# Seven block products in place of eight for the attention output of three tile groups, in a two-layer linear-attention and squared-ReLU kernel on one core

## The chip, the cores and the metric

The kernel runs on one core of a Trainium2 chip. The metric is device time in microseconds (us); lower is better. The time of a version is the median of several runs. Work is spread over TensorE (PE; its weight loads are shown apart as PEld), VectorE (DVE), ScalarE (ACT), GpSimd (POOL), and SyncE (SP), which issues nearly all DMAs.

## What is computed

```python
for layer in range(2):                                  # x: 2048 x 640, float32
    q, k, v = heads(layernorm(x) @ wqkv)                # 32 heads of 20
    pq, pk = phi(q), phi(k)                             # phi(t) = where(t > 0, t + 1, exp(t)) + 1e-6
    kv, z = sum_s(pk * v), sum_s(pk)                    # per head
    x = x + ((pq @ kv) / (pq @ z + 1e-6)) @ wo
    h = relu(layernorm(x) @ w1 + b1) ** 2               # 640 -> 1728
    x = x + h @ w2 + b2                                 # 1728 -> 640
```

## The kernel before, in words

The 2048 rows are 16 tiles of 128 rows; four tiles are a **group** g (four groups). Every float32 matrix is kept as a high and a low part, so each block of a matrix product is three matmuls of 128x128 on the weight side: high by low, low by high, high by high.

**First part of a layer.** A loop over the tiles t (lines 823 to 959) computes k and q features and collects, in PSUM, the sum G of x-transposed times k over all tiles. The strips of G for tile t-1 are worked off inside iteration t by `gs(n)` (line 883): line 894 does two of them right after the first block of features of tile t, and they need `kh` of tile t-1, the low half of which is written by DVE at line 793. In layer 0, lines 829 to 834 also store the split weights of k and q to DRAM (`keep_kq`, ten stores of 640 KB) in iterations 11 to 15; layer 1 loads them again. After the loop, G, the block-diagonal per-head kv and wo are multiplied into one 640x640 matrix **M**, kept as five row chunks `M[0..4]` of 128 rows. The attention output of a tile is then P_t @ M, where P_t is pq of the tile divided by its denominator.

**Second part: groups.** For each group, `fc1(g, c)` (line 1189) runs for c = 0..13, each 15 matmuls with 512 moving columns (10 for c = 13), and `act` (line 1210) makes relu squared on ACT. Then 28 `fc2_step`s follow (line 1273): seven block products of a Strassen-Winograd scheme, `ORDER`, of four steps each. Step n reads the n-th unit of the arena, a ring of five slots: ACT writes its high half (`u_hi`, line 1254), DVE the low half (`u_lo`, line 1261), one step after ACT, three steps ahead of PE. DVE also makes the sums of quadrants (`s_op`) and adds the products to the rows (`fc2_add`, line 1295).

**What sets the order.** Work beside the matmuls is put into `events` by hand: `at(g, n, f)` runs f after place n of group g, where n < 14 is an fc1 and n = NF + s an fc2 step s; `("pe", c)` runs PE work right after fc1(c). Each engine works its own queue off in that order. While group g runs, `single(g, i)` (line 1352) prepares tile t = 4(g+1)+i, one of the next group. With b = `OUTS[i]` (4, 7, 10, 13): load pq (`b_load_pq`, place b-8), denominators (`b_den`, b-6: a product and a reduction on DVE), division and transpose (`b_blocks`, b-5), sixteen small block moves on ACT (`blocks_move`, line 449: eight at b-5 and eight at b-4), the split into `pTs` (`p_split`, high on ACT, low on DVE, b-3 and b-2), then the 30 matmuls with M after fc1(b) into banks 6 and 7 (`out`), the add to the rows and layer norm statistics (b+1), the normed rows sent out through a POOL DMA (b+2), and the bias added on POOL (`f_bias`, b+3). Places below 0 go to the fc2 steps of group g-1, at two steps for one.

**Weights.** The weights of fc1 and fc2 come from DRAM through a ring of six 640 KB buffers (`Units`, line 331): a buffer is loaded again as soon as PE has used it. Tiles tagged "f" rotate through eight buffers.

Of the kernel before, what the change touches and what calls it, by code (L numbers as in the profile page):

```python
# [8 lines left out]
F32 = mybir.dt.float32  # L9
# [43 lines left out]
F_BUFS, X_BUFS = 8, 5  # L53
OUTS = (4, 7, 10, 13)


# [9 lines left out]
def kernel(  # L66
# [140 lines left out]

    uses = []
    for g in range(NG):
        uses += [(g, "w1", c) for c in range(NF)]  # L210
        uses += [(g, m, k) for m in ORDER for k in range(1, PAIRS)]

    def unit_len(nm, c):
        if nm == "w1":
            return 2 * D if c < 13 else DC * P
        a, b = unit_range(c)
        return 2 * HD * (b - a)
# [7 lines left out]
    for m in ORDER:  # L225
        for k in range(PAIRS):
            a, b = unit_range(k)
            keep((m, k), [P, 2, b - a, HD])

    class Prep:  # L230
# [100 lines left out]
    class Units:  # L331


        def __init__(self, short):
            self.at = {}
            self.ring = list(uses)
# [29 lines left out]
        def used(self, g, nm, c):  # L366
            if nm == "w1" or c > 0 or (g, nm, c) == self.moved:
                self.free += 1

        def get(self, g, nm, c):  # L370
            at_ring = nm == "w1" or c > 0 or (g, nm, c) == self.moved
            return self.at[(g, nm, c) if at_ring else (nm, c)]
# [70 lines left out]

    def blocks_T(src):
        y = ftile("y")
        nc.vector.transpose(out=y, in_=src)  # L446
        return [y]
# [100 lines left out]
    for layer in range(N_LAYERS):  # L548
# [153 lines left out]
        dens, xTb = {}, {}  # L702
        wu = Units(layer < N_LAYERS - 1)

# [17 lines left out]
        def b_ops(t):  # L722

            pr = ftile("pr")
            nc.vector.tensor_tensor(out=pr, in0=pq[t], in1=zbc, op=ALU.mult)
# [14 lines left out]
            yield  # L740
            yzp[t] = blocks_T(pq.pop(t))

# [80 lines left out]
        for t in range(NT):  # L823
# [159 lines left out]
        def late_rest(n=9):  # L983
            for _ in range(min(n, len(late_todo))):
                t, j = late_todo.pop(0)
                late_phi[t].rest()
                if j == 1:
                    nc.sync.dma_start(pqd[t], late_phi.pop(t).r)

        late_q(2)  # L990
        zbc = tmp.tile([P, D], F32, tag="z", name="zbc", bufs=1)
# [194 lines left out]
        arena = tmp.tile([P, SLOTS, 2, 2, HT], R32, tag="T", name="arena", bufs=2)  # L1186
        pTs = wtile("pTs").rearrange("p (b j n) -> p b j n", b=2, j=2)

# [163 lines left out]
        def single(g, i):  # L1352

            t, b = TG * (g + 1) + i, OUTS[i]

            def on(n, f):
                if n < 0 and g > 0:
                    at(g - 1, NF + N_STEPS + 2 * n, f)
                elif n >= NF:
                    at(g, NF + int(2 * (n - NF)), f)  # L1360
                else:
                    at(g, max(n, 0), f)

            if t > TG:
# [26 lines left out]

            def store():
                xn[t] = ftile("xn")
                ln_apply(("b", t), xn[t], xr[t])
                xd[t] = spread_out(xn.pop(t))

            at(g, ("pe", b), out)
            on(b + 1 + 0.5 * (i == 3), add)
            on(b + 2, store)
            on(b + 3, lambda: f_bias(t))  # L1400

            def load():
# [3 lines left out]
            at(g, NF + (0, 3, 7, 11)[i], load)  # L1406
            steps(lambda: x_split(t), (g, n + 4), (g, n + 5), (g, n + 6))

        def ffn_events(g):
# [67 lines left out]
        for t in range(TG):  # L1477
            at(0, 4 + 2 * t, lambda t=t: f_bias(t))
        for g in range(NG):
            ffn_events(g)  # L1480
        for g in range(NG - 1):
            for i in range(TG):
                single(g, i)
# [61 lines left out]
```

## Time and profile before

| | |
|---|---|
| runs | 1319.78, 1320.56 (median), 1321.46 us |
| the profiled execution | 1320.5 us, of which the profile's span covers 1318.5 us |
| TensorE, busy | 1310.7 us (99%) |
| VectorE, ScalarE, GpSimd, busy | 865.5 (66%), 735.5 (56%), 219.1 us (17%) |
| first part of layer 0, of layer 1 | up to 255.5 us; 656 to 907 us |
| groups of layer 0 | begin at 255.5, 361.9, 468.3 and 574.7 us |
| groups of layer 1 | begin at 906.9, 1013.3, 1119.7 and 1226.1 us |
| one whole group | 64.1 us of fc1 with four attention outputs, then 42.2 us of fc2 |

Times inside the span are counted from its start. A row of a timeline reads: start, duration, engine, line, operation, output <- inputs, shape, count, and in square brackets how long the engine sat idle before it and what ended that. Durations of matmuls in such rows overlap by the depth of TensorE's pipeline, so the pace is read from starts, or from the chain of waits.

### The profile page before, as it was taken

How to read it: one execution, taken by the hardware profiler on the slowest of the kernel's cores; microseconds unless marked ns; L12 is line 12 of the kernel's file. 1: busy time of each engine (PE TensorE's matmuls, PEld its weight loads, DVE VectorE, ACT ScalarE, POOL GpSimd, SP SyncE). 2: the span in 40 equal slices, each digit the busy share in tenths (PEclk: the TensorE clock that was granted, in tenths of full speed). 3: DMA queues.
4: the chain of work that ended last, by engine and by line, in shares of the span. 5: the costliest groups of instructions: out<-in, count | busy, mean ns of one | idle time of the engine just before them, and what ended most of it. 6: DMA issues, size and time to landing. Idle time of an engine off the chain costs nothing.

```text
span 1318.5 us, 20882 instructions
## 1 busy us (share of the span) xinstructions
PE 1310.7 (99%) x7477; PEld 1193.5 (91%) x7477; DVE 865.5 (66%) x1575; ACT 735.5 (56%) x1594; POOL 219.1 (17%) x289
## 2 busy tenths in 40 slices
PE   9999999999999999999999999999999999999998
PEld 8888889989988988998988889999899899889888
DVE  7888958767944954833856677686577559449045
ACT  5888967785475467334322233387844744854242
POOL 2333310064012002101012222001320120120000
PEclk9999999999999999999999999999999999999999
DMA  6898994499974985898954456454869659749756
GB/s 194 247 278 270 336 339 144 152 353 388 320 290 154 302 298 171 267 361 290 361 158 126 123 145 169 124 199 171 315 214 345 212 192 320 290 149 297 286 186 219
DMA packets 135036, 321.57 MB, mean 244 GB/s; under 512 B 16710, under 2 KB 61894, under 8 KB 134294
## 3 DMA queue, kind: packets, MB, share of 16 engines
q1 hardware_dynamic: 127702, 297.96, 67.1%
q0 software_dynamic: 7232, 22.29, 6.4%
q8 instruction: 59, 0.97, 0.3%
q14 instruction: 43, 0.35, 0.1%
HBM read 242.82 MB, written 65.54 MB: 234 GB/s over the span
## 4 chain that ended last, share of the span: by engine, by line
PE 91%; ACT 2%; DVE 2%; DMA 2%; SPq 1%; issue 1%; POOL 0%; ACTq 0%; DVEq 0%; POOLq 0%
PE PS L489 32%; PE PS L1204 28%; PE PS L1287 25%; PE PS L516 3%; ACT z L475 1%; PE PS L1042 1%; PE PS L1055 1%; DMA kq<-kept_kq 1%; SPq L246 1%; PE PS L849 0%; PE PS L637 0%; DMA xt<-in_A_x_dram 0%; DMA kept<-uprep 0%; DVE xT L505 0%; DVE r L599 0%
## 5 line engine op out<-in xcount | busy, mean ns | idle before, releaser
L1204 PE MATMUL PS<-xTb,u 128*128 128x512 f32 x1640 | 376.6, 389 | 0.0
L1204 PEld LDWEIGHTS PS<-xTb,u 128*128 128x128 f32 x1640 | 306.8, 188 | 62.5
L489 PE MATMUL PS<-kq,xT 128*128 128x320 f32 (+2 forms) x1575 | 285.0, 334 | 1.6 <-DVE xT L505 1.4
L489 PEld LDWEIGHTS PS<-kq,xT 128*128 128x128 f32 x1575 | 250.2, 188 | 29.8 <-DVE xT L505 2.2
L1287 PE MATMUL PS<-u,arena 128*128 128x320 f32 x1644 | 250.2, 309 | 0.0
L1287 PEld LDWEIGHTS PS<-u,arena 128*128 128x128 f32 x1644 | 243.4, 188 | 0.0
L1268 DVE TENSOR_TENSOR arena<-R,arena 128x512 fp32r<-128x512 f32 (+1 forms) x200 | 140.8, 707 | 135.3 <-ACT arena L1259 134.8
L1259 ACT ACTIVATE arena<-R 128x512 fp32r<-128x512 f32 (+1 forms) x200 | 117.9, 593 | 157.9 <-PE PS L1287 131.9
L455 ACT ACTIVATE z<-y 32x160 f32<-32x160 f32 x512 | 171.1, 334 | 49.8 <-DVE y L446 42.2
L1215 ACT ACTIVATE R<-PS,b1sb 128x512 f32<-128x512 f32 x104 | 71.5, 687 | 127.8 <-PE PS L1204 126.9
L489 PE MATMUL PS<-kh,xh 128*128 128x512 f32 x480 | 124.8, 393 | 1.0 <-DVE kh L793 0.9
L383 POOL TENSOR_SCALAR rs<-mv 128x1 f32<-128x1 f32 x64 | 34.9, 546 | 513.8 <-DVE mv L381 513.8
L489 PE MATMUL PS<-uM,pTs 128*128 128x320 f32 x720 | 109.4, 309 | 0.0
L489 PEld LDWEIGHTS PS<-uM,pTs 128*128 128x128 f32 x720 | 107.5, 188 | 1.9
L1287 PE MATMUL PS<-uw,arena 128*128 128x320 f32 x660 | 106.1, 309 | 0.0
L489 PEld LDWEIGHTS PS<-kh,xh 128*128 128x128 f32 x480 | 87.1, 188 | 16.9 <-DVE kh L793 1.8
L1287 PEld LDWEIGHTS PS<-uw,arena 128*128 128x128 f32 x660 | 99.2, 188 | 0.4 <-DVE x L1301 0.2
L1233 DVE TENSOR_TENSOR R<-R 128x512 f32<-128x512 f32 (+1 forms) x128 | 79.5, 626 | 26.0 <-ACT R L1216 26.0
L475 ACT ACTIVATE z<-y 32x160 f32<-32x160 f32 x272 | 90.9, 334 | 3.3
L591 ACT ACTIVATE r<-PS 128x512 f32<-128x512 f32 (+1 forms) x64 | 27.7, 434 | 99.4 <-PE PS L489 98.1
L1216 ACT ACTIVATE R<-R 128x512 f32<-128x512 f32 x104 | 65.8, 633 | 3.3
L598 DVE TENSOR_SCALAR r<-r 128x512 f32<-128x512 f32 (+1 forms) x64 | 21.3, 332 | 70.4 <-ACT r L591 70.2
(135 smaller groups left out, 1318.1 us busy)
## 6 DMA issues: line engine op xcount, KB each, us to landing
u<-kept SPq DMA_DIRECT2D x113, 640.0 KB, 5.6
u<-kept_w SPq DMA_DIRECT2D x104, 640.0 KB, 6.2
u<-kept SPq DMA_DIRECT2D x56, 320.0 KB, 6.1
kept<-uprep SPq DMA_DIRECT2D x49, 320.0 KB, 5.6
z<-xb SPq DMA_DIRECT2D x160, 80.0 KB, 5.3
pqt<-pq SPq DMA_DIRECT2D x32, 320.0 KB, 6.7
acc<-r POOLq DMA_DIRECT2D x28, 320.0 KB, 4.9
uw<-kept SPq DMA_DIRECT2D x14, 640.0 KB, 7.4
```

The source lines that it names most:

```text
L383: nc.gpsimd.tensor_scalar(rs, mv[:, 1:2], LN_EPS, None, op0=ALU.add)
L455: nc.scalar.activation(zv[j * B32 : (j + 1) * B32, :, i, :], yv[i * B32 : (i + 1) * B32, :, j, :], AF.Copy)
L475: nc.scalar.activation(zv[j * B32 : (j + 1) * B32, :, i, :], yv[i * B32 : (i + 1) * B32, j], AF.Copy)
L489: nc.tensor.matmul(ps, a, b, start=first and i == 0, stop=last and i == 2)
L516: nc.tensor.matmul(ps[:, j * 512 : j * 512 + HD], aT[:, k, c, :], w[c][:, l, j * HD : (j + 1) * HD], start=c == 0 and (k, l) == (1, 0), st ...
L1204: nc.tensor.matmul(ps, a[:, d, :], bb[:, d, :], start=(d, i) == order[0], stop=(d, i) == order[-1],)
L1215: nc.scalar.activation(r, v, AF.Relu, bias=b1sb[:, c : c + 1])
L1216: nc.scalar.activation(r, r, AF.Square)
L1233: nc.vector.tensor_tensor(out=quad(*out, k), in0=quad(*x, k), in1=quad(*y, k), op=op)
L1259: nc.scalar.activation(u[:, 0], v, AF.Copy)
L1268: nc.vector.tensor_tensor(out=u[:, 1], in0=v, in1=u[:, 0].bitcast(F32), op=ALU.subtract)
L1287: nc.tensor.matmul(ps, x, y, start=opens and k == 0 and p == 0 and e == 0, stop=k == PAIRS - 1 and p == b - a - 1 and e == len(seq) - 1, s ...
```

## The change

For group 3 in layer 0 (prepared during group 2) and groups 2 and 3 in layer 1 (prepared during groups 1 and 2), the four calls of `single` give way to `pairs(g)`: two tiles are stacked into a 256x640 matrix and multiplied by M in one level of the same seven-product scheme. Of M, chunks 0 to 3 form four quadrants of 256x320; chunk 4 is multiplied in the plain way. Per pair, seven products of 6 matmuls and four plain ones of 3 take the place of 60 matmuls. Six pairs are done so in all.

- `mix_M(g)`, one group earlier (group 1 in layer 0, group 0 in layer 1), makes the four mixed quadrants of M: adds of the two halves on DVE, sums on POOL, splits on ACT and DVE, eight stores of 320 KB in all on SP. One quadrant, `m5`, overwrites the right half of chunks 0 and 1; `m4`, `m6`, `m7` are loaded through the weight ring, three loads of 640 KB per pair.
- `pair(g, j)` begins at c0 = 0 or 6. Both tiles' transposed rows are changed in place by DVE sums (`s_op`), split quarter by quarter into four slots, multiplied after fc1(c0+4) to fc1(c0+7), and each product is added to the rows separately by DVE.
- The division, transpose and block moves stand at `MOVES_AT` = -3, -1, 2, 5 instead of b-5 = -1, 2, 5, 8, so two tiles are prepared in the fc2 steps of the group before. `b_ops` writes its transpose into the buffer of its product.
- In layer 0, t = 2, and in layer 1, t = 1, the two G strips of line 894 stand behind the second block of features. The ten `keep_kq` stores stand behind the loop, among the making of M and the first outputs.

```diff
+MOVES_AT, PAIR_AT = (-3, -1, 2, 5), (0, 6)
+MIX_G = (1, 0)
...
+                if MIX_G[layer] < g < NG - 1:
+                    for j, c0 in enumerate(PAIR_AT):
+                        if c0 + 5 <= c <= c0 + 7:
+                            uses.append((g, ("m6", "m7", "m4")[c - c0 - 5], j))
...
-                if t >= NT - DC:
-                    for j in range(2):
-                        keep_kq(t - NT + DC, j)
...
-            gs(0 if is_late or t == 1 and layer == 0 else 2)
+            gs(0 if is_late or t + layer < 3 else 2)
...
+            if t + layer == 2:
+                gs(2)
             if gt and not is_late:
...
+        run_keep(2)
         late_q(2)
...
+            if i % 2 == 0:
+                run_keep(1)
...
+        run_keep(2)
         for i in range(2):
...
             b_load_x(i + 2)
+            run_keep(2)
...
+        def pair(g, j):
+            on, c0 = after(g), PAIR_AT[j]
+            order = (1, 5, 6, 2, 7, 3, 4)
+            bk = {1: 4, 6: 4, 7: 4, 4: 4, 5: 5, 3: 5, 2: 6, "d": 7}
...
+            def begin():
+                for h in range(2):
+                    z[h] = yzp.pop(t0 + h)[1]
+                hi(1)
+                for h in range(2):
+                    nc.scalar.activation(rest4[:, h, 0], z[h][:, c4], AF.Copy)
...
+            on(c0 + 1, begin)
+            for n, ops in (
+                (2, ((lo, 1), (s_op, 1), (hi, 5))),
+                (3, ((lo, 5), (s_op, 2), (hi, 6), (hi, 2))),
+                (4, ((lo, 6), (lo, 2), (s_op, 3), (s_op, 4), (hi, 7), (hi, 3))),
+                (5, ((lo, 7), (lo, 3), (hi, 4))),
+                (6, ((lo, 4),)),
+            ):
+                for f, m in ops:
+                    on(c0 + n, lambda f=f, m=m: f(m))
+            on(c0 + 2, rest_lo)
+            plan = ((1, 5, "d"), (6, 2), (7, 3), (4,))
+            for i, ms in enumerate(plan):
+                for m in ms:
+                    at(g, ("pe", c0 + 4 + i), lambda m=m: product(m))
+            yield
+            for i, ms in enumerate(plan):
+                for m in ms:
+                    on(c0 + 4 + i, lambda m=m: add(m))
+            for h in range(2):
+                on(c0 + 6 + h, lambda h=h: ln_stats(("b", t0 + h), xr[t0 + h]))
+                on(c0 + 7 + h, lambda h=h: norm_out(t0 + h))
+            for h in range(2):
+                on(c0 + 9, lambda h=h: f_bias(t0 + h))
...
+            for i, b in enumerate(MOVES_AT):
+                t = TG * (g + 1) + i
+                on(b - 4, lambda t=t: b_load_pq(t))
+                on(b - 1, lambda t=t: b_den(t))
+                on(b, lambda t=t: b_blocks(t))
+                on(b, lambda t=t: blocks_move(yzp[t], (0, 1)))
+                on(b + 1, lambda t=t: blocks_move(yzp[t], (2, 3)))
...
+            for c, f, p in (
+                (0, whole, 0), (0, mix, 0), (2, high, 0), (3, low, 0), (3, store, 0), (3, whole, 1),
+                (3, mix, 1), (5, high, 1), (6, low, 1), (6, store, 1),
+            ):
+                at(g, c, lambda f=f, p=p: f(p))
+            for p in range(2):
+                at(g, NF + 4 + 4 * p, lambda p=p: place(p))
```

Three places of the queues, each before and then after; lines are those of each version's own file.

ACT, from the last fc2 steps of group 1 of layer 0 into group 2. `arena` rows of 64x256 are a high half of an fc2 step (the last one for step 27), `z<-y` are block moves, `R` rows the two operations of `act`, `pTs` rows the high halves of the attention input. Before:

```order
L1259 ACTIVATE arena<-R 128x512 x3
L1257 ACTIVATE arena<-R 64x256
L455 ACTIVATE z<-y 32x5x32 x8
L1215 ACTIVATE R<-PS,b1sb 128x2x256
L1216 ACTIVATE R<-R 128x2x256
L455 ACTIVATE z<-y 32x5x32 x8
L1215 ACTIVATE R<-PS,b1sb 128x2x256
L1216 ACTIVATE R<-R 128x2x256
L1315 ACTIVATE pTs<-z 128x640
```

After:

```order
L1284 ACTIVATE arena<-R 128x512 x3
L469 ACTIVATE z<-y 32x5x32 x8
L1282 ACTIVATE arena<-R 64x256
L469 ACTIVATE z<-y 32x5x32 x16
L1240 ACTIVATE R<-PS,b1sb 128x2x256
L1241 ACTIVATE R<-R 128x2x256
L469 ACTIVATE z<-y 32x5x32 x8
L1240 ACTIVATE R<-PS,b1sb 128x2x256
L1241 ACTIVATE R<-R 128x2x256
L1469 ACTIVATE pTs<-z 128x256
L1480 ACTIVATE pTs<-z 128x128 x2
```

Eight block moves now stand ahead of the high half for step 27, and 32 instead of 16 stand ahead of the first split of the group.

DVE, around the first attention output of group 2 of layer 0. `x_3025<-PS` rows add a product to the rows; `pr` or `y<-pqt,zbc` and the reduction are the denominators of a later tile. Before:

```order
L725 TENSOR_TENSOR pr<-pqt,zbc 128x640
L728 TENSOR_REDUCE den<-pr 128x32
L1389 TENSOR_TENSOR x_3025<-PS,x_3025 128x320 x2
L379 BN_STATS bn<-x_3025 128x6 x2
L381 BN_AGGR mv<-bn 128x2
```

After, from the low half of product 5 to the first adds of block products:

```order
L1473 TENSOR_TENSOR pTs<-z,pTs 128x256
L1466 TENSOR_TENSOR z<-z 128x256
L1473 TENSOR_TENSOR pTs<-z,pTs 128x256 x2
L1466 TENSOR_TENSOR z<-z 128x256 x2
L739 TENSOR_TENSOR y<-pqt,zbc 128x640
L742 TENSOR_REDUCE den<-y 128x32
L1531 TENSOR_TENSOR x_3025<-PS,x_3025 128x320 x3
```

The first of the three adds, of product 1, now stands behind two low halves, two sums and a denominator; PE's product 6 adds onto the same bank and waits for it.

POOL, at the end of fc1 of group 2 of layer 0. `rs` rows are the layer norm's root, `xb<-xn` sends normed rows out, `x_3025` rows are bias adds. Before:

```order
L383 TENSOR_SCALAR rs<-mv 128x1
L384 TENSOR_TENSOR rs<-rs,neghalf 128x1
L417 DMA xb<-xn 128x640
L1185 TENSOR_TENSOR x_3025<-x_3025,b2bc 128x640
L383 TENSOR_SCALAR rs<-mv 128x1
L384 TENSOR_TENSOR rs<-rs,neghalf 128x1
L417 DMA xb<-xn 128x640
L1185 TENSOR_TENSOR x_3025<-x_3025,b2bc 128x640
```

After:

```order
L396 TENSOR_SCALAR rs<-mv 128x1
L397 TENSOR_TENSOR rs<-rs,neghalf 128x1
L430 DMA xb<-xn 128x640
L396 TENSOR_SCALAR rs<-mv 128x1
L397 TENSOR_TENSOR rs<-rs,neghalf 128x1
L430 DMA xb<-xn 128x640
L1209 TENSOR_TENSOR x_3025<-x_3025,b2bc 128x640 x2
```

The bias adds of the last two tiles now stand together behind the last send, which in the program is fc2 step 2.

More of the change, by code (lines that the diff above doesn't have):

```diff
@@ L205, in wk, with uses_of @@
         return [kq[c][:, :, s] for c in range(DC)]
[L208 to L211, printed above, removed]
+    def uses_of(layer):
+        uses = []
+        for g in range(NG):
+            for c in range(NF):
+                uses.append((g, "w1", c))
+                if MIX_G[layer] < g < NG - 1:
+                    for j, c0 in enumerate(PAIR_AT):
+                        if c0 + 5 <= c <= c0 + 7:
+                            uses.append((g, ("m6", "m7", "m4")[c - c0 - 5], j))
+            uses += [(g, m, k) for m in ORDER for k in range(1, PAIRS)]
+        return uses
     def unit_len(nm, c):
+        if nm in ("m4", "m6", "m7"):
+            return 2 * D
         if nm == "w1":
@@ L228 @@
             keep((m, k), [P, 2, b - a, HD])
+    for m in ("m4", "m5", "m6", "m7"):
+        kept[m, 1] = keep((m, 0), [P, 2, 2, HD])
     class Prep:
@@ L331, with __init__ @@
     class Units:
-        def __init__(self, short):
+        def __init__(self, uses, short):
             self.at = {}
-            self.ring = list(uses)
+            self.ring = uses
             self.moved = (NG - 1, ORDER[-1], 0) if short else None
@@ L440, in turn, with blocks_T @@
         return y
-    def blocks_T(src):
-        y = ftile("y")
+    def blocks_T(src, y=None):
+        if y is None:
+            y = ftile("y")
         nc.vector.transpose(out=y, in_=src)
@@ L702 @@
         dens, xTb = {}, {}
-        wu = Units(layer < N_LAYERS - 1)
+        wu = Units(uses_of(layer), layer < N_LAYERS - 1)
         def b_load_pq(t):
@@ L988, in late_rest, with run_keep @@
                     nc.sync.dma_start(pqd[t], late_phi.pop(t).r)
+        keeps = [(c, j) for c in range(DC) for j in range(2)] if layer == 0 else []
+        def run_keep(n):
+            for _ in range(min(n, len(keeps))):
+                keep_kq(*keeps.pop(0))
+        run_keep(2)
         late_q(2)
@@ L1186 @@
         arena = tmp.tile([P, SLOTS, 2, 2, HT], R32, tag="T", name="arena", bufs=2)
-        pTs = wtile("pTs").rearrange("p (b j n) -> p b j n", b=2, j=2)
+        wt = wtile("pTs")
+        pTs = wt.rearrange("p (b j n) -> p b j n", b=2, j=2)
         def fc1(g, c):
@@ L1354, in single @@
             t, b = TG * (g + 1) + i, OUTS[i]
[L1356 to L1362, printed above, removed]
+            on = after(g)
             if t > TG:
@@ new lines, in pairs @@
+        def pairs(g):
+            on = after(g)
+            both = [pair(g, j) for j in range(2)]
+            for p in both:
+                next(p)
+            for i, b in enumerate(MOVES_AT):
+                t = TG * (g + 1) + i
+                on(b - 4, lambda t=t: b_load_pq(t))
[3 more added lines that the diff above has]
+                on(b + 1, lambda t=t: blocks_move(yzp[t], (2, 3)))
+                on(PAIR_AT[i // 2] + 1, lambda t=t: b_load_x(t))
+                x_in(g, i)
+            for p in both:
+                next(p, None)
@@ L1478 @@
             at(0, 4 + 2 * t, lambda t=t: f_bias(t))
+        mix_M(MIX_G[layer])
         for g in range(NG):
@@ L1481 @@
         for g in range(NG - 1):
+            if g > MIX_G[layer]:
+                pairs(g)
+                continue
             for i in range(TG):
```

134 lines of the change are left out of this document (125 added, 9 removed).

## Prediction

> **What bounds the kernel now.** I read the page's busy times and chain first, then who PE waits for, then busy times by stage.
>
> ```profile
> PE 1310.7 (99%) x7477; PEld 1193.5 (91%) x7477; DVE 865.5 (66%) x1575; ACT 735.5 (56%) x1594; POOL 219.1 (17%) x289
> ...
> PE 91%; ACT 2%; DVE 2%; DMA 2%; SPq 1%; issue 1%; POOL 0%; ACTq 0%; DVEq 0%; POOLq 0%
> ```
>
> ```profile
> PE PS L489 <- DVE xT L505: 1.4, 2, 1.2
> PE PS L637 <- POOL ident masks.py:199: 1.4, 1, 1.4
> PE PS L489 <- DVE kh L793: 0.9, 2, 0.5
> PE PS L489 <- DMA kq<-kept_kq: 0.2, 1, 0.2
> ```
>
> PE bounds it: 99% busy, 91% of the chain, and under 4 us of waits in all, none of them in the groups. So every matmul removed is time gained, and every wait added is time lost. The question is whether the engines that feed PE keep up. By stage (busy time and count of PE, PEld, DVE, ACT, POOL; granted clock; DMA share; GB/s):
>
> ```profile
> 195.00:226.00 31.00, 31.00 (x206) 27.41 (x205) 23.97 (x47) 23.28 (x58) 0.00 (x0) 1.00 0.47 140
> ...
> 255.50:319.70 64.20, 64.20 (x328) 56.12 (x327) 43.54 (x71) 48.56 (x109) 30.21 (x31) 1.00 0.95 352
> 426.10:468.30 42.20, 42.20 (x289) 42.20 (x288) 37.75 (x66) 15.78 (x27) 3.33 (x5) 1.00 0.89 286
> 468.30:532.40 64.10, 64.10 (x326) 56.02 (x326) 29.28 (x55) 43.97 (x100) 10.39 (x12) 1.00 0.66 233
> ```
>
> In fc1 (last row) DVE works 29 of 64 us; in fc2 (third row) 37.75 of 42.2. The change gives DVE more to do on both sides of that second stage.
>
> Durations come from the profiled execution, 1320.5 us, which is the median of the runs (1320.56) to 0.1 us.
>
> **Matmuls removed.** The chain of waits in group 2 of layer 0, fc1 and one output:
>
> ```profile
> 459.94 8.36 PE PS L1287 x57
> 468.30 17.02 PE PS L1204 x75
> 485.32 4.39 PE PS L489 x30
> ```
>
> The 30 matmuls of an output take 4.39 us, 0.146 each; the fc2 ones, with weights from the ring, take 8.36/57 = 0.147, so `m4`, `m6`, `m7` cost no other pace. A pair has 7 x 6 + 4 x 3 = 54 matmuls in place of 60; six pairs save 36, or **5.3 us**. The Trainium skill ("TensorE: Matmul & The Clock Gate", Back-to-back issue gap) gives a sustained 81 ns at 128 columns and 131 at 512; an estimate between them is 106 ns at 320, which would make the saving 3.8 us. The trace has 146 at 320 and 17.02/75 = 227 at 512, so it disagrees and decides.
>
> **Strips moved.** Timeline of PE:
>
> ```profile
> 30.98 3.56 PE L489 MATMUL PS<-kq,xT 128*128 128x512 f32 x15
> 35.03 1.66 PE L489 MATMUL PS<-kh,xh 128*128 128x512 f32 x6 [0.48 <-DVE kh L793]
> ```
>
> ```profile
> 665.88 10.27 PE L489 MATMUL PS<-kq,xT 128*128 128x512 f32 x51 [0.21 <-DMA kq<-kept_kq]
> 676.58 1.67 PE L489 MATMUL PS<-kh,xh 128*128 128x512 f32 x6 [0.42 <-DVE kh L793]
> ```
>
> At 0.227 each the block of 30.98 is over at 34.38, and the strips start at 35.03: 0.65 lost, pipeline included. The 51 of the second pair (36 of 512 columns, 15 of 256 at half the pace) are over by 675.8, strips at 676.58: 0.75. The next block of features needs only `xT` of its own tile, which was there, and by its end (3.4 us on) the low half is too. I take **1.4 us** gained; bounds 0 and 1.4.
>
> **k and q stores.** Cost nothing where they go: DMA is busy 0.47 there (first stage row), PE never waits. Ten of 640 KB are 6.6 MB, 19 us at the 352 GB/s of the second row; without that cover a late load could cost a few us. Where they leave, the two waits on `xT` (1.4 us in all) end with DVE behind ACT's moves, not with a DMA; I take 0, the bound is 1.4 gained.
>
> **Added loads and stores.** Per pair group 6 x 640 KB come to 233 GB/s x 64.1 us = 14.9 MB: 18.9 MB in 62.3 us, 303 GB/s. The second stage row ran 352 without a wait of PE, so I take 0.
>
> **Queues at the start of a pair group.** This is where the order shown ahead decides. DVE and ACT now, at the turn to group 2:
>
> ```profile
> 457.69 0.49 DVE L1301 TENSOR_TENSOR x<-PS,x 128x320 f32<-128x320 f32 x1
> 458.10 0.68 DVE L1268 TENSOR_TENSOR arena<-R,arena 128x512 fp32r<-128x512 f32 x1
> ...
> 459.10 0.68 DVE L1268 TENSOR_TENSOR arena<-R,arena 128x512 fp32r<-128x512 f32 x1
> ...
> 464.10 0.83 DVE L725 TENSOR_TENSOR pr<-pqt,zbc 128x640 f32<-128x640 f32 x1 [1.27 <-DMA pqt<-pq]
> ...
> 466.10 0.17 DVE L734 TENSOR_SCALAR den<-den 128x32 f32<-128x32 f32 x1
> ...
> 467.55 0.84 DVE L446 STREAM_TRANSPOSE y<-pqt 128x640 f32<-128x640 f32 x1
> ```
>
> ```profile
> 461.44 0.42 ACT L1257 ACTIVATE arena<-R 64x256 fp32r<-64x256 f32 x1 [0.69 <-PE PS L1287]
> 468.43 2.77 ACT L455 ACTIVATE z<-y 32x160 f32<-32x160 f32 x8 [6.57 <-DVE y L446]
> 471.76 0.69 ACT L1215 ACTIVATE R<-PS,b1sb 128x512 f32<-128x512 f32 x1 [0.56 <-PE PS L1204]
> ...
> 473.12 2.75 ACT L455 ACTIVATE z<-y 32x160 f32<-32x160 f32 x8
> 475.90 0.69 ACT L1215 ACTIVATE R<-PS,b1sb 128x512 f32<-128x512 f32 x1
> ```
>
> ```profile
> L1268 DVE TENSOR_TENSOR arena<-R,arena 128x256 fp32r<-128x256 f32 x32 | 15.1, 472 | 18.6 <-ACT arena L1259 18.6
> L1259 ACT ACTIVATE arena<-R 128x256 fp32r<-128x256 f32 x32 | 13.1, 410 | 9.1 <-PE PS L1287 7.6 <-DVE R L1233 1.5
> ```
>
> From these: denominators 1.65 us, division and transpose 2.3 (466.10 to 468.39), eight moves 2.78 (473.12 to 475.90), `act` 1.3 (471.76 to 473.12), a quarter's split 0.4 on ACT and 0.4 on DVE. Laid end to end in the new order, on the clock of this trace: the first tile's denominators run from 458.1 to 459.75, two low halves and an add to 461.35, its transpose to 463.65, its moves on ACT to 466.45, and the high half of step 27 behind them ends at 466.9 instead of 461.86, its low half at 467.3. Step 27 begins at 468.30 - 4 x 0.147 = 467.7: just in time. DVE goes on with an add, the second tile's denominators, an add and its transpose (4.7) until 472.0. From there ACT has no pause: moves, `act`, moves, `act`, first split and rest, `act`, split of product 5: 10.6, until 482.6; DVE's transpose of the third tile is over at 484.05; moves, `act`, the splits of 6 and 2 until 488.9. DVE then has a low half, two sums, denominators and the add of product 1: about 3.1, until 492.0. PE wants product 6 at 468.30 + 17.02 + 15 x 0.146 + 3.40 = 490.9. So PE **waits 1.1 us** here, with all of fc1 queued behind it, in each of three groups: **3.3 us**. Bounds 0 and 2.2 each: two rounds of moves, two transposes and three `act` lie in this chain, and a fifth of it (2.2 of some 28 us) is as far as I trust the sum.
>
> **DVE in fc2 after a pair group.** DVE, POOL, DVE and PE, each from its timeline:
>
> ```profile
> 430.28 2.68 DVE L1268 TENSOR_TENSOR arena<-R,arena 128x512 fp32r<-128x512 f32 x1 [0.54 <-ACT arena L1259]
> ```
>
> ```profile
> 430.14 0.64 POOL L417 DMA_DIRECT2D xb<-xn  x1 [1.56 <-DVE xn L389]
> 430.81 1.59 POOL L1185 TENSOR_TENSOR x<-x,b2bc 128x640 f32<-128x640 f32 x1
> ```
>
> ```profile
> 437.18 0.65 DVE L1268 TENSOR_TENSOR arena<-R,arena 128x512 fp32r<-128x512 f32 x1
> ```
>
> ```profile
> 439.97 2.22 PE L1287 MATMUL PS<-u,arena 128*128 128x320 f32 x14
> ```
>
> A low half that takes 0.68 took 2.68 while POOL added a bias. Now two bias adds stand there, and the last rows' norm, which waits for POOL, stands ahead of the low half of step 5, with 3.1 us less between fc1's end and fc2. Now over 432.96 - 426.06 = 6.9 us into fc2 (426.06 is 42.24 ahead of 468.30), that low half would be over at 8.2 by the same reckoning, and the operations behind it meet the second add (1.59): DVE is 1.4 us late (if transposes and waits take the second add) to 3.0 (if two-input operations do); I take 2.0, a little under the middle, because DVE still idles there now (0.54 in the row) and can take up some of it. Step 9's low half ends at 437.83, PE begins at 439.97: 2.1 us of cover, the same at steps 13, 17 and 21. So 2.0 hides, unless a pair group follows: there (group 1 to 2 of layer 1) DVE has no idle left, and the chain above ends **2.0 us** later. The Trainium skill ("SBUF — State Buffer", Who interferes with whom) says that a VectorE operation with two SBUF inputs and a GpSimd operation that reads SBUF exclude each other for a whole instruction, and that whichever starts first goes on. The trace agrees on the first; on the second the record of DVE begins 0.53 ahead of POOL's, and DVE still ends 0.57 behind it.
>
> **Mixing M.** 14 us of DVE and POOL work in a stage with room, save one place: in layer 1 the first output of group 0 has little lead.
>
> ```profile
> 920.44 0.83 DVE L1317 TENSOR_TENSOR pTs<-z,pTs 128x640 fp32r<-128x640 f32 x1 [2.01 <-ACT pTs L1315]
> ```
>
> ```profile
> 923.97 4.39 PE PS L489 x30
> ```
>
> ```profile
> L269 POOL TENSOR_TENSOR wa<-wq,wa 128x320 f32<-128x320 f32 x5 | 4.4, 884 | 0.4
> ```
>
> The lead is 923.97 - 921.27 = 2.7. Ahead of it come two DVE adds (1.6) and, alternating with DVE, four POOL sums (0.88 each), about 2.7 together: I take **0.2** lost, bounds 0 and 1.
>
> **Sum:** -5.3 - 1.4 + 3.3 + 2.0 + 0.2 = -1.2; 1320.5 - 1.2 = **1319.3 us**. Gains at most 8.1 with no new wait: 1312.4; all waits at their upper ends (6.6, 3.0 and 2 x 0.9 for DVE, 1): 12.4 against 6.7 or less, 1326.2.
>
> **Rivals.**
> - *The queues keep up.* If ACT starts the first group's moves 1 us sooner than laid out and POOL's second add falls on DVE's waits, both terms go: 1320.5 - 6.7 + 0.2 = 1314.0, and with half of them left 1316.6. For it: the trace shows DVE idle 1.27 us waiting for a load that is now issued six steps ahead. Against it: that idle is in the sum, and the moves are serial.
> - *DVE sets fc2's pace, slower.* Late by L us, DVE costs PE L - 2.1 in each fc2 after a pair group, and L in the chain to group 2 of layer 1. With 3.5 of the other waits and 6.7 of gains, time rises above 1323.1 once 3L - 4.2 is over 5.8, L = 3.3; at L = 4 it is 1325.1. For it: 90% busy DVE. Against: L must exceed its upper end of 3.0.
> - *The ring starves.* Stores of mixed M block SP until DVE has made their data. A buffer is wanted six uses later, over 12 us; this needs SP held longer than 6 us, and costs some 3 us per group: 1325 or more.
> - *The products save nothing* (other pace): 1324.6.
>
> **Chances.** Forecast 0.43 (1317.9 to 1323.1, that is within 0.2% or 2.6 us, about what a measurement can tell from no change); queues keep up 0.36; DVE's pace 0.14; ring 0.05; pace 0.02. So faster 0.36, same 0.43, slower 0.21; range 1314.5 to 1324.5, with about a tenth left out at each end.
>
> **What would show it.** PE has 7441 matmuls at 0.146 each in the outputs. Waits of PE on the add of product 1 after fc1(5), about 1 us in three groups, and some 3 us together at group 2 of layer 1, would prove the chain; none there, the first rival. Waits on `arena` low halves around steps 9 to 21 of fc2 behind a pair group would prove the second; on ring loads the third. The waits on `kh` must be gone at 35 and 676 us. Wrong from the start would be PE idle in places that no term names.

## The result and the profile after

The changed kernel takes **1324.49 us** (median of 10 runs, 1321.03 to 1326.43) beside 1320.35 us for the kernel before (10 runs, 1319.78 to 1321.46): ratio 1.0031, 95% interval 1.0022 to 1.0039. It is 4.1 us slower where 1.2 us less was forecast. Its profiled execution took 1323.54 us, 1321.8 of it in the span; this is 3.3 us more than the span of before, and these 3.3 are accounted for below.

The page of the changed kernel, busy times and shares of the chain:

```profile
PE 1307.9 (99%) x7441; PEld 1187.8 (90%) x7441; DVE 916.8 (69%) x1685; ACT 746.1 (56%) x1648; POOL 236.2 (18%) x305
...
PE 71%; DVE 13%; ACT 8%; DMA 4%; issue 2%; SPq 1%; POOL 1%; DVEq 0%; ACTq 0%; POOLq 0%
```

The 36 matmuls are gone (7477 to 7441). PE is still "99% busy", yet its share of the chain fell from 91% to 71%, and DVE, ACT and DMA hold 25% where they held 6%: long stretches of the end time now run through the engines that feed PE. Whom PE waits for (total, times, longest):

```profile
PE PS L1520 <- ACT z L469: 3.8, 3, 1.3
PE PS L1312 <- DVE arena L1289: 2.9, 3, 1.2
...
PE PS L860 <- ACT kq L170: 0.4, 1, 0.4
PE PS L503 <- DVE pTs L1342: 0.3, 1, 0.3
```

The two waits on `kh` of before are gone; two kinds of wait are new, three times each. L1520 is a block product, L1312 an fc2 step, L1289 the low half of a 64-row fc2 step, here step 27. The rows of PE at the three turns into a pair group:

```profile
468.23 0.85 PE L1312 MATMUL PS<-u,arena 128*128 128x320 f32 x4 [0.55 <-DVE arena L1289]
...
492.98 1.12 PE L1520 MATMUL PS<-u,pTs 128*128 128x320 f32 x6 [1.26 <-ACT z L469]
...
1014.36 0.85 PE L1312 MATMUL PS<-u,arena 128*128 128x320 f32 x4 [1.10 <-DVE arena L1289]
...
1039.11 1.11 PE L1520 MATMUL PS<-u,pTs 128*128 128x320 f32 x6 [1.27 <-ACT z L469]
...
1122.62 0.86 PE L1312 MATMUL PS<-u,arena 128*128 128x320 f32 x4 [1.24 <-DVE arena L1289]
...
1147.37 1.11 PE L1520 MATMUL PS<-u,pTs 128*128 128x320 f32 x6 [1.25 <-ACT z L469]
```

The weights `u` of the L1520 rows come from the ring, so this is product 6, as forecast. The list puts its wait down to ACT's moves, but those are of the next pair's tiles, and product 6 reads nothing of them: it reuses the PSUM bank of product 1, and DVE's add of product 1 (L1531) began at 492.40. From the late step 27 to product 6 it is 24.75 us in all three groups (492.98 - 468.23 and so on). Two waits that keep a constant distance are links of one chain. Its beginning, on ACT and then on DVE:

```profile
464.52 2.76 ACT L469 ACTIVATE z<-y 32x160 f32<-32x160 f32 x8 [3.80 <-DVE y L460]
467.31 0.42 ACT L1282 ACTIVATE arena<-R 64x256 fp32r<-64x256 f32 x1
467.75 2.75 ACT L469 ACTIVATE z<-y 32x160 f32<-32x160 f32 x8
...
472.93 2.77 ACT L469 ACTIVATE z<-y 32x160 f32<-32x160 f32 x8 [2.42 <-DVE y L460]
```

```profile
455.11 0.84 DVE L449 STREAM_TRANSPOSE y<-z 128x640 f32<-128x640 f32 x1 [1.19 <-DMA z<-xb]
...
458.35 0.49 DVE L1326 TENSOR_TENSOR x<-PS,x 128x320 f32<-128x320 f32 x1
458.98 0.83 DVE L739 TENSOR_TENSOR y<-pqt,zbc 128x640 f32<-128x640 f32 x1
...
463.64 0.85 DVE L460 STREAM_TRANSPOSE y<-pqt 128x640 f32<-128x640 f32 x1
...
467.76 0.42 DVE L1289 TENSOR_TENSOR arena<-R,arena 64x256 fp32r<-64x256 f32 x1 [2.70 <-ACT arena L1282]
...
468.62 0.81 DVE L739 TENSOR_TENSOR y<-pqt,zbc 128x640 f32<-128x640 f32 x1
...
472.05 0.84 DVE L460 STREAM_TRANSPOSE y<-pqt 128x640 f32<-128x640 f32 x1
...
492.40 1.47 DVE L1531 TENSOR_TENSOR x<-PS,x 128x320 f32<-128x320 f32 x3
```

ACT's first eight moves stand ahead of the high half of step 27 (467.31). DVE needs that half for its low half, idles 2.70 us for it, and the second tile's denominators (468.62) stand behind that low half in DVE's queue. ACT then idles 2.42 us for the second tile. If this is one chain, one instruction in the wrong place makes PE wait twice; e1 and e5 below ask for that.

The whole account goes by the length of a group, from its first fc1 matmul to that of the next (0/1 is group 1 of layer 0). These are differences of rows of PE's timeline. The labels are those of the experiments:

| us | 0/1 | 0/2, pairs | 1/0 | 1/1, pairs | 1/2, pairs |
|---|---|---|---|---|---|
| before | 106.38 | 106.39 | 106.39 | 106.39 | 106.38 |
| changed | 107.20 | 106.30 | 108.37 | 108.27 | 106.33 |
| e1, high half first | 106.38 | 104.82 | 106.99 | 105.59 | 105.17 |
| e5, denominators first | 108.36 | 104.82 | 108.84 | 106.79 | 104.86 |
| e6, the fastest | 106.39 | 104.81 | 106.39 | 105.28 | 105.19 |
| e9, e6 without bias adds | 106.39 | 104.71 | 106.85 | 104.96 | 104.71 |

Step 27's wait falls into the group before a pair group, product 6's into the pair group. The five groups of the changed kernel are 4.54 us longer in sum; from the last group of layer 0 to layer 1's groups it is 0.80 shorter (the strips), and the end 0.4: 3.3.

### The profile page after: what moved, and what is told of

The parts are those of the page before. It is cut to its first block, busy times and chain, and to the rows that moved or that the text cites. A ratio compares the mean times of both kernels' runs of the same rounds, so it can differ in the third digit from the quotient of the medians.

```text
span 1321.8 us, 21111 instructions
## 1 busy us (share of the span) xinstructions
PE 1307.9 (99%) x7441; PEld 1187.8 (90%) x7441; DVE 916.8 (69%) x1685; ACT 746.1 (56%) x1648; POOL 236.2 (18%) x305
## 4 chain that ended last, share of the span: by engine, by line
PE 71%; DVE 13%; ACT 8%; DMA 4%; issue 2%; SPq 1%; POOL 1%; DVEq 0%; ACTq 0%; POOLq 0%
PE PS L503 27%; PE PS L1229 20%; PE PS L1312 16%; ACT z L469 4%; PE PS L1520 3%; DVE arena L1293 2%; PE PS L530 2%; DVE R L1258 2%; ACT z L489 2%; PE PS L1064 1%; PE PS L1077 1%; DVE x L1326 1%; DVE pqt L751 1%; DVE y L460 1%; DMA uw<-kept 1%
## 5 line engine op out<-in xcount | busy, mean ns | idle before, releaser
L1312 PE MATMUL PS<-u,arena 128*128 128x320 f32 x1644 | 251.6, 309 | 2.9 <-DVE arena L1289 2.9
L1312 PEld LDWEIGHTS PS<-u,arena 128*128 128x128 f32 x1644 | 243.4, 188 | 4.3 <-DVE arena L1289 3.7
L1293 DVE TENSOR_TENSOR arena<-R,arena 128x512 fp32r<-128x512 f32 (+1 forms) x200 | 143.9, 724 | 84.7 <-ACT arena L1284 84.3
L1312 PE MATMUL PS<-uw,arena 128*128 128x320 f32 x660 | 106.2, 309 | 0.0
L1312 PEld LDWEIGHTS PS<-uw,arena 128*128 128x128 f32 x660 | 99.2, 188 | 0.5 <-DVE x L1326 0.2
L1258 DVE TENSOR_TENSOR R<-R 128x512 f32<-128x512 f32 (+1 forms) x128 | 88.4, 694 | 14.8 <-ACT R L1241 14.8
L1326 DVE TENSOR_TENSOR x<-PS,x 128x320 f32<-128x320 f32 x112 | 53.1, 482 | 18.6 <-PE PS L1312 17.9
L503 PE MATMUL PS<-uM,pTs 128*128 128x320 f32 x360 | 55.0, 309 | 0.3 <-DVE pTs L1342 0.3
```

Of the source, the lines that this page charges most:

```text
L503: nc.tensor.matmul(ps, a, b, start=first and i == 0, stop=last and i == 2)
L1258: nc.vector.tensor_tensor(out=quad(*out, k), in0=quad(*x, k), in1=quad(*y, k), op=op)
L1293: nc.vector.tensor_tensor(out=u[:, 1], in0=v, in1=u[:, 0].bitcast(F32), op=ALU.subtract)
L1312: nc.tensor.matmul(ps, x, y, start=opens and k == 0 and p == 0 and e == 0, stop=k == PAIRS - 1 and p == b - a - 1 and e == len(seq) - 1, s ...
L1326: nc.vector.tensor_tensor(out=v, in0=ps, in1=v, op=ALU.add)
```

## The experiments

Each was timed in five rounds beside the kernel before on the same chip, whose median was 1320.30 us for e1 to e4, 1320.25 for e5 to e7, 1320.02 for e8 and e9, and 1320.16 for e10 and e11. The theory is the single chain; its rivals are two separate waits, ScalarE's serial moves, and DVE late in fc2.

**e1: the high half of step 27 ahead of the moves.**

```diff
-                on(b, lambda t=t: blocks_move(yzp[t], (0, 1)))
+                on(b + 0.5 * (i == 0), lambda t=t: blocks_move(yzp[t], (0, 1)))
```

> Changed kernel, but ScalarE makes the high half of step 27 ahead of the first tile's first eight block moves (nothing else moves). In the trace of the changed kernel VectorE idles 2.70 us for that half with the second tile's denominators queued behind it, PE waits for its low half three times (the starts of fc1 come 0.8, 1.4 and 1.5 us late) and for the first product's add three times (1.26, 1.27, 1.25 us idle, about 1.5 with the pipeline). Theory A, one chain: the half behind the moves delays both, so the second tile's moves come about 2.3 us sooner, the three waits for step 27 go, and those for the add go in layer 0 and shrink to about 0.5 in the two groups of layer 1: 7.1 us, 1317.4. Rival B, two separate waits: only those for step 27 go, the products still wait 1.3 each: 1320.8. Rival C, the end of the chain is set elsewhere (VectorE late in fc2): what step 27 gives back the add takes: 1324.5, with the add's waits at 2 us or more.

Measured: **1316.14 us** (ratio 0.9971, 0.9960 to 0.9983), 8.3 less than the changed kernel and faster than before. PE's list holds neither L1520 nor L1312 any more. ACT and DVE at the same turn:

```profile
461.20 0.42 ACT L1282 ACTIVATE arena<-R 64x256 fp32r<-64x256 f32 x1 [0.69 <-PE PS L1312]
463.13 5.54 ACT L469 ACTIVATE z<-y 32x160 f32<-32x160 f32 x16 [1.51 <-DVE y L460]
468.87 2.76 ACT L469 ACTIVATE z<-y 32x160 f32<-32x160 f32 x8 [0.21 <-DVE y L460]
```

```profile
463.70 0.42 DVE L1289 TENSOR_TENSOR arena<-R,arena 64x256 fp32r<-64x256 f32 x1
...
464.56 0.81 DVE L739 TENSOR_TENSOR y<-pqt,zbc 128x640 f32<-128x640 f32 x1
...
468.00 0.84 DVE L460 STREAM_TRANSPOSE y<-pqt 128x640 f32<-128x640 f32 x1
...
488.34 1.47 DVE L1531 TENSOR_TENSOR x<-PS,x 128x320 f32<-128x320 f32 x3
```

The half is done in a gap that ACT has anyway, before the first transpose is over, so the moves lose nothing; DVE does not idle for it; from the first transpose (462.25 here, 463.64 in the changed kernel) to the add of product 1 it takes 26.1 us in place of 28.8. Two separate waits (1320.8) and an end set elsewhere (1324.5) are both out. The one chain was expected to leave 0.5 us of the product wait in each group of layer 1 (1317.4); nothing of it is left.

**e5: the second tile's denominators ahead of the low half.** This parts the two links: ACT's order stays as in the changed kernel, and only what queues behind DVE's idle time is taken from there.

```diff
-                on(b - 1, lambda t=t: b_den(t))
+                on(b - 1 - 0.5 * (i == 1), lambda t=t: b_den(t))
```

> Changed kernel, but VectorE makes the second tile's denominators (product and reduction) one step earlier, so that they stand ahead of the low half of step 27, in the 2.70 us for which VectorE idles there; ScalarE's order is that of the changed kernel, with the high half of step 27 behind eight moves. In the changed kernel the time from that low half to the first product's add is the same in all three groups (PE restarts 24.75 us apart each time), one rigid chain. Theory: the harm to the products is that the second tile's denominators queue behind the low half; now division, transpose and moves of the second tile come 1.6 us sooner, the wait for the add (1.26 and the pipeline's fill, some 1.5) goes in three groups, the waits for step 27 stay (0.55, 1.10, 1.24): 1324.5 - 4.5 = 1320.0. Rival: the product waits come from ScalarE's serial moves alone, VectorE has time: no change, 1324.5.

Measured: **1319.11 us** (0.9992, 0.9983 to 1.0001). One line of PE's list, and DVE at the first turn:

```profile
PE PS L1312 <- DVE arena L1289: 3.7, 3, 1.2
```

```profile
466.37 0.81 DVE L739 TENSOR_TENSOR y<-pqt,zbc 128x640 f32<-128x640 f32 x1
467.22 0.82 DVE L742 TENSOR_REDUCE den<-y 128x32 f32<-128x640 f32 x1
469.16 0.42 DVE L1289 TENSOR_TENSOR arena<-R,arena 64x256 fp32r<-64x256 f32 x1 [1.12 <-ACT arena L1282]
...
471.87 0.85 DVE L460 STREAM_TRANSPOSE y<-pqt 128x640 f32<-128x640 f32 x1
```

The product waits are gone although ACT's moves stand as before, and step 27's stay (1.24 each in this run). So what delays the products is what stands behind the low half on DVE. Pair groups come down to 104.82 and 104.86; against 106.30 and 106.33 that is 1.47 for the product wait with the refill of PE's pipeline behind it. Groups 0/1 and 1/0 are longer than in the changed kernel: in this execution, which is 1.5 us above the run's median, DVE idled 1.71 and 1.57 us for the transposed rows, where the changed kernel's profile has 1.19 and 1.35.

**e2 and e11: the loads of m5 later.**

```diff
-                at(g, NF + 4 + 4 * p, lambda p=p: place(p))
+                at(g, NF + 13 + 4 * p, lambda p=p: place(p))
```

> Changed kernel, but the two loads of m5 into M stand at steps 13 and 17 of fc2 in place of 4 and 8, behind the last loads of transposed rows. In the trace of the changed kernel those rows land late in the two groups with the loads (VectorE idles 1.19 and 1.35 us for them, not at all in the kernel before). Theory: the two loads in front of them on SP are the cause; both idle times go, the chain to the next group starts 1.2 us sooner in two groups and PE waits 1.2 less in each: 1322.1. Rival: SP is late because of the ring (loads of fc2 and fc1 weights that wait for a buffer), not because of these two: idle times stay, 1324.5. Rival: the idle time is hidden by ScalarE's serial moves: the idle goes, the time stays at 1324.5.

> The kernel of e2 once more (loads of m5 at steps 13 and 17), beside e10 on the same chip, since the changed kernel itself scatters over 5.4 us and this one over 1.7: 1323.0, and the same small scatter, if the scatter comes from when the rows behind the early loads of m5 land; a scatter of 4 us or more, if not.

Measured: 1323.02 us (1.0021, 1.0012 to 1.0030) and 1323.07 (1.0022, 1.0013 to 1.0032), 1.4 to 1.5 less than the changed kernel where 2.4 were expected, and with overlapping runs. In the profiled executions groups 0/1 and 1/0 together are 0.4 us shorter in e2 and 0.7 in e11. DVE at the first turn of e2:

```profile
454.20 0.85 DVE L449 STREAM_TRANSPOSE y<-z 128x640 f32<-128x640 f32 x1 [0.20 <-DMA z<-xb]
...
458.82 0.83 DVE L739 TENSOR_TENSOR y<-pqt,zbc 128x640 f32<-128x640 f32 x1 [0.89 <-DMA pqt<-pq]
```

The idle time for the rows falls from 1.19 to 0.20, but DVE then idles 0.89 for `pqt`, the next load in SP's order, and the denominators begin at 458.82 in place of 458.98. A moved load of m5 now stands ahead of this `pqt`, which SP issues at 452.51 in place of 452.01. In the traces most of the gain went to that next wait. The changed kernel has it too: its add in front of the denominators ended at 458.84, and DVE then idled 0.15 for `pqt`. Nor is m5 the only cause of the late rows: at this turn DVE idled 0.21 to 1.71 us for them in the six executions with the loads at steps 4 and 8, and 0 to 0.49 in the five with steps 13 and 17. The 0.21 is of e1, where nothing but ACT's order differs from the changed kernel. The expectation on the scatter failed: e2 ran from 1322.07 to 1323.81, the same kernel as e11 from 1320.90 to 1325.67.

**e3: bias adds moved into the next group.**

```diff
-                on(c0 + 9, lambda h=h: f_bias(t0 + h))
+                at(g + j, (9, 10 + h)[j], lambda h=h: f_bias(t0 + h))
```

> Changed kernel, but GpSimd's two bias adds of the second pair are not made in the first fc2 steps, but after fc1(10) and fc1(11) of the next group. In the trace of the changed kernel two VectorE operations beside the two adds take 2.10 and 1.80 us in place of 0.68 and 0.41. Theory: that is what makes VectorE some 1.5 us late on the way into group 2 of layer 1, the only place where such an fc2 is followed by a pair group: 1.5 to 1.8 us gained, 1322.9. Rival: VectorE takes it up in its idle time before the end of fc2: within 0.3 of the changed kernel, 1324.3. Rival: the adds do the same harm where they now stand: 1324.5 or more, with stretched operations beside fc1(10).

Measured: 1325.33 us (1.0041, 1.0027 to 1.0055), slower than before; the 0.8 beside the changed kernel lies within the scatter (1324.19 to 1327.27 here, 1321.03 to 1326.43 there). Group 1/1 came down from 108.27 to 107.53, but 1/2 went up from 106.33 to 109.81, where four adds now stand together. POOL, DVE and PE there, and PE's stretch behind (busy times and counts of PE, PEld, DVE, ACT, POOL; granted clock; DMA share; GB/s):

```profile
1163.77 6.13 POOL L1209 TENSOR_TENSOR x<-x,b2bc 128x640 f32<-128x640 f32 x4
```

```profile
1163.82 6.63 DVE L1293 TENSOR_TENSOR arena<-R,arena 128x512 fp32r<-128x512 f32 x1 [1.13 <-ACT arena L1284]
```

```profile
1171.45 1.44 PE L1520 MATMUL PS<-uM,pTs 128*128 128x320 f32 x8 [1.75 <-DVE pTs L1473]
```

```profile
1173.00:1176.50 3.50, 3.50 (x10) 2.78 (x9) 3.21 (x8) 1.31 (x4) 0.00 (x0) 0.52 0.00 0
1176.50:1180.00 3.50, 3.50 (x23) 3.24 (x22) 0.49 (x1) 2.01 (x4) 0.00 (x0) 1.00 0.31 79
```

A VectorE operation of 0.68 us was held for all four adds, and with it a split that a product needs: about 2 us of the 3.5. The rest is TensorE itself. Behind that wait its granted clock was 0.52 over 3.5 us, and eight matmuls of fc1 came 0.43 us apart in place of 0.23: 1.6 us. So the whole 3.5 is not the price of the adds' place alone; whether the other runs of e3 lost the clock too is not shown. Half of the theory's gain came in 1/1, and the last rival (harm where the adds now stand) took more than that.

**e8 and e10: the adds left out.** The same two adds are not made at all, in the changed kernel (e8) and in e2 (e10).

```diff
-            for h in range(2):
+            for h in range(2 if j == 0 else 0):
                 on(c0 + 9, lambda h=h: f_bias(t0 + h))
```

> Changed kernel without the bias adds of the second pair's two tiles (leaves out b2 for these six tiles' rows), so that no GpSimd add stands beside VectorE in the fc2 behind a pair group. Asks for the prediction's term of 2.0 us (VectorE late in that fc2, which counts at the turn to group 2 of layer 1). The prediction: 2.0 gained, 1322.5. From the run with the two adds moved into the next group: the step-27 wait at that turn went only from 1.24 to 1.06, and VectorE there idled 0.39, 0.51 and 0.86 us for the loads of transposed rows, so the loads take the adds' place: 0.2 to 0.4 gained, 1324.2.

> The kernel of e2 without the two bias adds of the second pair (leaves out b2 for these rows). The prediction's term: 2.0 less than e2, at the turn to group 2 of layer 1. From the trace of the run without them (group 1 of layer 1 0.78 us shorter, of it 0.20 at step 27): 0.8 less than e2. Rival: the loads of rows take the adds' place wholly: within 0.3 of e2.

Measured: 1321.76 us (1.0013, 1.0003 to 1.0022), and 1319.70 (0.9998, 0.9989 to 1.0007), 2.7 less than the changed kernel and 3.4 less than e11. Both are more than the expectations (0.2 to 0.4, and 0.8) and nearer to the prediction's 2.0, though each of these kernels scatters by 3.3 to 5.8 us. Group 1/1 is 107.49 and 107.80 (108.27 to 108.28 in the changed kernel, e2 and e11), 0/2 and 1/2 are 0.1 shorter each: 0.7 to 1.0 in the traces. POOL and DVE with the adds, in the changed kernel (the second row of POOL is the second add alone):

```profile
1085.32 3.59 POOL L1209 TENSOR_TENSOR x<-x,b2bc 128x640 f32<-128x640 f32 x2
1086.86 2.05 POOL L1209 TENSOR_TENSOR x<-x,b2bc 128x640 f32<-128x640 f32 x1
```

```profile
1085.37 2.10 DVE L1258 TENSOR_TENSOR R<-R 128x512 f32<-128x512 f32 x1
1087.39 1.80 DVE L1293 TENSOR_TENSOR arena<-R,arena 128x256 fp32r<-128x256 f32 x1
```

Two operations of 0.68 and 0.41 take 3.90: DVE is 2.8 late, inside the 1.4 to 3.0 of the prediction. Without the adds DVE idles 0.5 to 1.1 us at a time for loads of rows and of `pqt` instead, and PE gets back less than a third of it by the groups' lengths. The medians say more than the profiled executions account for. In both runs group 1/0, which the edit does not touch, was also shorter (107.32 and 107.00 beside 107.84 to 108.37 in the changed kernel, e2 and e11). Why is open.

**e4: the strips alone, on the kernel before.**

```diff
-            gs(0 if is_late or t == 1 and layer == 0 else 2)
+            gs(0 if is_late or t + layer < 3 else 2)
...
+            if t + layer == 2:
+                gs(2)
```

> Kernel before with the two early G strips moved behind the second block of features in both layers, and nothing else. The prediction: 0.65 + 0.75 = 1.4 us gained, 1318.95. From the trace of the changed kernel: only the 0.75 of layer 1 come through, since in layer 0 a later stretch of the loop waits for VectorE, ScalarE and loads, not for PE: 1319.6. Rival: nothing comes through: 1320.35.

Measured: 1318.98 us (11 runs, 0.9992, 0.9983 to 1.0001). PE in layer 0 and layer 1:

```profile
30.64 6.96 PE L489 MATMUL PS<-kq,xT 128*128 128x512 f32 x30
37.44 1.52 PE L489 MATMUL PS<-kh,xh 128*128 128x512 f32 x6
39.22 1.14 PE L489 MATMUL PS<-xh,kh 128*128 128x320 f32 x6 [0.25 <-DVE r L599]
```

```profile
663.28 15.66 PE L489 MATMUL PS<-kq,xT 128*128 128x512 f32 x75
678.78 2.20 PE L489 MATMUL PS<-kh,xh 128*128 128x512 f32 x9
```

The features run through and the strips follow without a wait. In layer 0 most of it comes back one operation later: 0.76 with the refill is gone, and 0.52 stands behind the strips (0.25 idle). So by the rows the strips give 0.2 there and 0.7 in layer 1, 0.9 together. The median is 1.3 lower, near the 1.4 forecast, though the interval touches no change. The agreement is in part luck: this execution was already 0.3 ahead in front of the strips of layer 0, and lacks the wait on `kept_kq` (0.48 with the refill) of the kernel before.

**e6, e7, e9: the best version, and what is left in it.** e7 is e1 with the first mix after fc1(1), e6 is e7 with the loads of m5 of e2, and e9 is e6 without the bias adds.

```diff
-                (0, whole, 0), (0, mix, 0), (2, high, 0), (3, low, 0), (3, store, 0), (3, whole, 1),
+                (1, whole, 0), (1, mix, 0), (2, high, 0), (3, low, 0), (3, store, 0), (3, whole, 1),
```

> Changed kernel with three edits: the high half of step 27 ahead of the moves (as in e1), the loads of m5 at steps 13 and 17 (as in e2), and the first mix of M after fc1(1) in place of fc1(0), behind the first tile's denominators and transpose. e1 alone gave 1316.1. Theory: with no wait left at the turns, the loads of m5 change nothing; the mix gives back the wait of the first output of layer 1 (0.33 us idle, 0.6 with the pipeline): 1315.5. Rival: the mix later makes its stores and the second mix late, DVE's work at fc1(6) and (7) collides with fc2's first halves: 1316.5 or more.

> As e6, but with the loads of m5 where the changed kernel has them (steps 4 and 8): high half of step 27 ahead of the moves, first mix of M after fc1(1). Theory: 1315.5, as e6, since the idle time that the loads of m5 cause VectorE is not on the path any more. Rival: the idle time still counts in layer 1: 0.3 to 1 us more than e6.

> The fastest version so far (e6: high half of step 27 ahead, m5 loads later, first mix later; 1315.4) without the same two bias adds per pair group (leaves out b2 for these rows). In e6 the pair groups of layer 1 last 105.28 and 105.19 us where the group of before less 12 matmuls would last 104.63, that of layer 0 104.81, and no wait over 0.2 us is on record; VectorE is busy 35.0 of 36.0 us in the fc2 behind (e1). Theory: the stretched operations beside the adds make low halves late by fractions, the groups of layer 1 come to 104.8 to 105.0: 0.6 gained, 1314.8. Rival: the rest is at the start of the products, nothing gained, 1315.4.

Measured: e6 **1315.39 us** (0.9964, 0.9951 to 0.9976), e7 1315.45 (0.9967, 0.9954 to 0.9979), e9 1313.95 (0.9955, 0.9943 to 0.9968). All that PE waits for in e6 was there before:

```profile
PE PS L503 <- DVE xT L519: 1.4, 2, 1.2
PE PS L651 <- POOL ident masks.py:199: 1.4, 1, 1.4
```

Group 1/0 falls from 106.99 (e1) to 106.39 in e6 and in e7, the length it had before, so the mix had cost 0.60. The loads of m5 change nothing once the chain is off the path. In e9 two pair groups last 104.71, or 1.67 below 106.38: the twelve matmuls at 0.146 (1.76) almost in full. Its median is 1.4 below e6 where 0.6 was expected; the spans of the two profiled executions differ by 0.7.

## Why the prediction was wrong, step by step

- **Matmuls removed**, 5.3: right. 1.67 of 1.76 per pair group shows once nothing waits (e9).
- **Strips**, 1.4: by the rows 0.9 (e4), since in layer 0 PE then waits for DVE's next result; that the median of e4 says 1.3 is in part luck. In the profile of the changed kernel layer 1 kept 0.80. Layer 0 kept only 0.03: the same 0.52 came back, and an earlier wait of 0.4 on ACT (L860) stands in that execution. **k and q stores, added loads:** no wait of PE on a ring load, as taken.
- **Queues at the start of a pair group**, +3.3: the mechanism and the place were right (product 6 waits for the add of product 1). Measured: 3 x 1.47 = 4.4, inside its range of 0 to 6.6.
- **Step 27 "just in time"**, +0: this is the step that failed. The first tile's denominators were set at 458.1, the clock of the trace of before, and step 27's low half then came out 0.4 us early (467.3 beside 467.7; the rows of before have step 27 at 467.55), priced at nothing and left out of the range. They began at 458.98, because DVE waited for two loads that the chain left out: 1.19 us for transposed rows, then 0.15 for the tile's own `pqt`. Either can use up the 0.4: with most of the first gone, e2 still began at 458.82. The low half was ready at 468.2, and PE lost 0.82 (107.20 - 106.38) there, 1.38 at the next turn (108.37 - 106.39, less 0.60 for the mix), and 2.08 at the third (108.27 - 104.71 - 1.47): 4.3 in all. In the third DVE's lateness from the bias adds is in it, and only some 1.5 of the 2.08 stand at step 27 itself; the rest are waits of 0.1 to 0.3 at earlier fc2 steps. With the high half first (e1), PE waits for step 27 at none of the turns, although the loads were late there too (1.48 us idle in 1/0).
- **DVE in fc2 after a pair group**, +2.0: DVE's lateness was inside its bounds (2.8 measured, 2.0 taken, 1.4 to 3.0 given), and hides elsewhere as said (0.1 in 0/2 and 1/2). Its price at the turn was too high: 0.5 to 0.8 by the groups' lengths, since without the adds DVE waits for loads instead. What the medians of e8 and e10 give beyond that is open.
- **Mixing M**, +0.2: mis-sized, 0.60 (e6 against e1), inside its bound of 1. The four POOL sums stretch more of DVE's operations than were counted: three beside them took 3.5 us in place of 1.8 in the changed kernel.

Together: -5.0 - 0.8 + 4.4 + 4.3 + 0.6 is +3.5, with 0.1 each from the adds in 0/2 and 1/2 it is 3.7, and the end of the kernel gives 0.4 back: the 3.3 of the spans. Of the 4.5 between this and the forecast's -1.2, step 27 makes 2.3 (4.3 less the 2.0 set for DVE's lateness at the third turn), the product waits 1.1, the strips in this execution 0.6, the mix 0.4, the matmuls 0.3; the small rest and the end cancel.

The first rival (queues keep up, 1314.0 to 1316.6) describes e1 and e6 well: the change does hold a gain, of which one instruction's place on ACT cost more than all. That rival was tied to ACT starting 1 us sooner; the runs show that the order on ACT mattered, not its load. The rival of DVE's pace needed 3.3 us of lateness where 2.8 came, the ring starved nowhere, and the products saved what they promised.

## What to carry to other kernels

Where a chain is laid out and one link comes out "just in time" by less than a wait that the trace already shows on that engine, give it a price and a range, and look whose loads were put ahead of the chain's on the issuing queue. Before new work goes ahead of a short instruction, ask who waits for that instruction and what queues behind the waiter: here 2.8 us of moves ahead of a 0.4 us copy reached PE twice. When two waits keep a constant distance in every group, look for the one link ahead of both.

## What the runs showed of the hardware

- **One VectorE operation was held for four GpSimd adds** (e3: 6.63 us in place of 0.68; the adds took 6.13, back to back). The Trainium skill ("SBUF — State Buffer", Who interferes with whom) says that the one that issues first keeps the shared ports for its whole instruction. That agrees with the start (GpSimd's record is 0.05 ahead); that VectorE did not get its turn between GpSimd's instructions is what this trace adds. It is not so each time: beside two adds in the changed kernel the VectorE operation ended at 1087.47, while the second add, begun at 1086.86, took 2.05 in place of 1.6. What makes the difference is open.
- **TensorE's granted clock fell to half once behind a wait** (e3: 1.75 us idle, then 0.52 over 3.5 us, then 1.00 again). In the other kept traces it is 1.00 throughout, but for at most the last 1.5 us. That this wait brought it about is not shown; waits of up to 1.3 us in the other traces left the clock at 1.00.
- **The loads of rows land unevenly.** In eleven profiled executions of the changed kernel and its variants, on the way out of group 1 of layer 0, DVE's last transpose of rows began 27.98 to 30.60 us after the first fc2 matmul, with 0 to 1.71 us idle for the rows (28.58 in the kernel before, without a wait). Kernels whose chain to PE goes through these loads scatter by 1.7 to 5.8 us over 10 or 11 runs, the kernel before by 0.9 to 2.5 over 10 to 22, e4 by 0.7. That the landing makes the scatter is argued from this, not shown, and it is not all: from the start of the last group of layer 0 to that of layer 1's first, e11's execution took 333.09 us and the other kernels with the moved strips 331.0 to 331.7, with other waits.
